# Loading w_mod by contraction rows in two parts, with zero products for the clock allowed from the first loads on, in a fused attention and MLP kernel

## The chip, the cores and the metric

The kernel runs on one core of one Trainium2 chip. The metric is the device time of one execution in microseconds. A second figure in this text is the **span**, from the first to the last instruction of the profile or of a timed run's record; the time is about 1.8 us longer than it (862.16 us against 860.4 in the profiled run of the kernel before). Every timed run, apart from the first six of the kernel before, also carries the mean clock that the throttle granted TensorE over the span.

## The reference, cut to what matters

One transformer block: x is 2048 rows by 640, 32 heads of 20, an MLP of 1536. What the change touches is the start, where six modulation vectors come from one product with w_mod (640 x 3840), and the first two of them scale and shift the normalised x ahead of the q/k/v projection.

```python
mod = (_silu(c) @ w_mod).reshape(c.shape[0], 6, 1, -1)
sa, ca, ga, sb, cb, gb = (mod[:, 0].copy(), mod[:, 1].copy(), ...)     # cut
h = _layernorm(x, axis=-1) * (1 + ca) + sa
x = x + ga * _A_ref(h, A_wqkv, A_wo)          # attention
h = _layernorm(x, axis=-1) * (1 + cb) + sb
x = x + gb * _B_ref(h, B_w1, B_b1, B_w2, B_b2)   # MLP
```

## The kernel before

The program does not write its instruction streams by hand. It lists operations with estimated durations, a list scheduler in the file gives each a time in a model of the chip, and the streams are emitted in the order of those times. Two consequences matter here. A number such as the byte count given to a load is only the scheduler's guess: the transfer itself does not depend on it, the order does. And where PE would idle in the model, the scheduler puts in zero products (name "fill") to keep TensorE's clock up.

The parts concerned, with cuts marked:

```python
OKT, RB = 3, 300000
# ... in the scheduler: when to put in a zero product
thin = 30.0 < bt < self.flast and not any(x.name == "fill" for x in avail["pe"]) and \
    sum(x[1] for x in fl if x[0] > bt - self.TICK + 0.3) < FLOOR
# ... the first loads (last argument: the scheduler's guess of bytes)
dma("sp", xb[0][:, 0:2, :], xsrc(0, 256), 560000)
dma("sp", xb[0][:, 2:4, :], xsrc(256, 256), 400000)
dma("sp", wm0[:, :, 0:D], wmod_v[:, :, 0:D], 1350000)
for a, b in ((D, WS), (WS, 2 * D)):
    dma("sp", wm0[:, :, a:b], wmod_v[:, :, a:b], 1280 * (b - a))
# ... 50 products of one column each, c after SiLU is s_col
for m in range(10):
    for kt in range(KD):
        mm((bb if m < WM else bb_)[:, m:m + 1], wm0[:, kt, m * 128:(m + 1) * 128], s_col[:, kt:kt + 1],
           kt == 0, kt == KD - 1, 0, 1, cyc=130, name="mod")
# ... their sums go to modc / modc2, with 1 added to the scale
# ... then transposes of the normalised x, evacuated with scale and shift; projections; scores; exponentials
# ... GpSimd clears the padded output weights, over the first x buffer once it has been normalised
pool(lambda e: e.memset(wo_pad[:, g, :], 0.0), [wo_pad[:, g, :]], [negh], dur=0.56, prio=7)
```

The softmax here doesn't subtract the row's maximum and nothing guards it: scores larger than these inputs give would overflow.

## Time and profile before

| | kernel before |
|---|---|
| time, median of 3 runs | 860.66 us (860.4 to 861.09) |
| span of the profiled run, mean clock | 860.4 us, 0.998 |
| ScalarE, PE, VectorE busy | 95%, 97%, 93% |
| first exponential | 20.69 us |

The prediction below shows the page, the chain and the clock. Here are the two timelines of the start. Columns: start in us, duration in us, engine, line, operation, output from input, shapes, count, and in brackets the idle time ahead with what ended it. PE, from the timeline of 7 to 24 us of the kernel before:

```profile
10.32 0.78 PE L753 MATMUL psum<-arena 128*128 128x1 bf16 x25 [1.04 <-DMA arena<-in_w_mod_dram]
11.72 0.53 PE L753 MATMUL psum<-arena 128*128 128x1 bf16 x15 [0.61 <-DMA arena<-in_w_mod_dram]
12.74 0.40 PE L753 MATMUL psum<-arena 128*128 128x1 bf16 x10 [0.42 <-DMA arena<-in_w_mod_dram]
13.01 0.89 PE L759 MATMUL psum<-arena 128*128 128x128 bf16 x13
```

The three groups of one-column products each wait for one part of w_mod; the transposes follow in the same queue. VectorE over the same stretch:

```profile
11.03 1.31 DVE L912 TENSOR_SCALAR arena<-arena 128x640 bf16<-128x640 bf16 x2 [1.99 <-POOL arena L908]
```

The last two x tiles are normalised by 12.34 us, so with the third part landing at 12.7 the two inputs of the transposes come at nearly the same time.

### The profile page before, as it was taken

Reading aid. Unit: us, or ns where it says so; the run is one execution under the profiler, and the core shown is the slowest. Engines: PE = TensorE matmul, PEld = TensorE weight load, DVE = VectorE, ACT = ScalarE, POOL = GpSimd, SP = SyncE. Lnnn points to the kernel's source line nnn. Section 1 sums busy time; section 2 is a strip of 40 time slices with the busy share of each in tenths; the row PEclk is TensorE's granted clock in tenths of the full one; section 3 lists DMA queues with packets and bytes.
Section 4 is the critical chain, followed back from the end, with each engine's and each line's share of the span. In section 5 each row is a group of like instructions: output and inputs, shape, how many; then the busy total and the mean of one; then the engine's idle time right before and its main releaser. Section 6 shows DMA issues by size and latency. Waiting matters only on the chain.

```text
span 860.4 us, 16684 instructions
## 1 busy us (share of the span) xinstructions
PE 836.7 (97%) x6710; PEld 296.0 (34%) x6768; DVE 797.5 (93%) x1601; ACT 821.5 (95%) x898; POOL 194.7 (23%) x460
## 2 busy tenths in 40 slices
PE   8999999999999999999999999999999999999998
PEld 3433333332332222333233333233333322333466
DVE  6958999999999999999999999999999999899862
ACT  2999999999999999999999999999999999999982
POOL 4500100027010000199300551000017400000110
PEclk9999999999999999999999999999999999999999
DMA  8600000011010000510000100100100000000000
GB/s 272 183 3 2 26 13 14 14 46 58 15 33 12 14 14 17 189 49 14 12 5 20 37 22 22 44 10 23 32 22 15 14 14 2 20 29 24 8 2 32
DMA packets 29320, 30.02 MB, mean 35 GB/s; under 512 B 10938, under 2 KB 23610, under 8 KB 29242
## 3 DMA queue, kind: packets, MB, share of 16 engines
q1 hardware_dynamic: 29242, 28.94, 10.6%
q8 instruction: 53, 0.87, 0.4%
q14 instruction: 25, 0.20, 0.1%
HBM read 25.94 MB, written 2.87 MB: 33 GB/s over the span
## 4 chain that ended last, share of the span: by engine, by line
PE 48%; ACT 37%; DVE 12%; DMA 1%; issue 1%; SPq 0%; ACTq 0%
ACT arena L1049 35%; PE psum L753 18%; PE psum L1032 18%; PE psum L1096 9%; DVE arena L1059 3%; DVE arena L1065 3%; PE psum L840 3%; DVE arena L1062 2%; ACT arena L1402 1%; DMA arena<-in_w_mod_dram 1%; PE psum L759 1%; DVE arena L900 1%; DVE arena L959 1%; DVE arena L977 1%; DVE arena L1395 0%
## 5 line engine op out<-in xcount | busy, mean ns | idle before, releaser
L1049 ACT ACTIVATE arena<-psum 128x1024 bf16<-128x1024 f32 x845 | 779.4, 1105 | 4.4 <-PE psum L1032 3.8
L1032 PE MATMUL psum<-arena 32*128 32x512 bf16 (+2 forms) x2304 | 367.6, 359 | 9.3 <-DVE arena L1065 2.7
L753 PE MATMUL psum<-arena 128*128 128x320 bf16 (+6 forms) x1708 | 328.3, 300 | 8.3 <-issue 3.9
L1059 DVE TENSOR_SCALAR arena<-psum 128x512 f16<-128x512 uint16 x356 | 236.2, 680 | 14.4 <-PE psum L1032 12.7
L1065 DVE SCALAR_TENSOR_TENSOR arena<-psum,arena 128x512 uint16<-128x512 f32 x356 | 237.6, 679 | 2.5
L1032 PEld LDWEIGHTS psum<-arena 32*128 32x128 bf16 x2304 | 98.7, 91 | 266.8 <-ACT arena L1049 188.0
L1096 PE MATMUL psum<-arena 128*32 128x512 bf16 (+5 forms) x2304 | 181.7, 362 | 1.2 <-DVE arena L1104 0.7
L753 PEld LDWEIGHTS psum<-arena 128*128 128x128 bf16 (+1 forms) x1766 | 126.9, 97 | 159.1 <-issue 105.1
L1144 POOL TENSOR_TENSOR arena<-arena 128x128 bf16<-128x128 bf16 x122 | 52.9, 463 | 484.0 <-DMA arena<-scr 484.0
L1062 DVE TENSOR_TENSOR arena<-arena 128x512 f16<-128x512 f16 x356 | 149.1, 437 | 1.5
L1096 PEld LDWEIGHTS psum<-arena 128*32 128x32 bf16 (+1 forms) x2304 | 44.3, 93 | 90.4 <-issue 78.7
L840 PE MATMUL psum<-arena 128*128 128x512 bf16 (+3 forms) x230 | 74.1, 394 | 0.0
L1313 POOL TENSOR_TENSOR arena<-arena 128x128 bf16<-128x128 bf16 x105 | 44.7, 459 | 38.3 <-DVE arena L1228 37.8
L1370 POOL TENSOR_TENSOR arena<-arena 128x128 bf16<-128x128 bf16 x120 | 50.7, 453 | 10.0 <-DVE arena L912 10.0
L900 DVE BATCH_NORM_STATS2 arena<-arena 128x6 f32<-128x320 bf16 x96 | 43.6, 479 | 1.1 <-DMA arena<-in_A_x_dram 0.6
L907 POOL TENSOR_SCALAR arena<-arena 128x1 f32<-128x1 f32 (+1 forms) x40 | 9.6, 241 | 106.8 <-DVE arena L902 106.6
L840 PEld LDWEIGHTS psum<-arena 128*128 128x128 bf16 x230 | 19.5, 100 | 35.7 <-issue 29.0
L1415 DVE TENSOR_TENSOR arena<-psum,arena 128x320 bf16<-128x320 f32 x32 | 15.5, 484 | 14.1 <-PE psum L753 14.0
L1395 DVE TENSOR_SCALAR arena<-psum,arena 128x512 bf16<-128x512 f32 (+1 forms) x39 | 28.1, 720 | 0.1
L959 DVE TENSOR_SCALAR arena<-psum,arena 128x512 bf16<-128x512 f32 x31 | 23.0, 742 | 4.7 <-PE psum L753 4.7
L912 DVE TENSOR_SCALAR arena<-arena 128x640 bf16<-128x640 bf16 x48 | 23.2, 497 | 3.0 <-POOL arena L908 3.0
L1104 DVE CAST arena<-psum 128x512 bf16<-128x512 f32 (+2 forms) x36 | 22.3, 621 | 3.3 <-PE psum L1096 3.3
(57 smaller groups left out, 215.0 us busy)
## 6 DMA issues: line engine op xcount, KB each, us to landing
arena<-scr SPq DMA_DIRECT2D x29, 256.0 KB
arena<-in_A_x_dram SPq DMA_DIRECT2D x6, 640.0 KB, 4.5
arena<-in_B_w_dram SPq DMA_DIRECT2D x2, 1920.0 KB
arena<-in_w_mod_dram SPq DMA_DIRECT2D x2, 1600.0 KB
out_dram<-arena SPq DMA_DIRECT2D x16, 160.0 KB, 1.8
arena<-in_A_wqkv_dram SPq DMA_DIRECT2D x3, 800.0 KB
arena<-in_A_x_dram SPq DMA_DIRECT2D x4, 320.0 KB
arena<-in_w_mod_dram SPq DMA_DIRECT2D x1, 800.0 KB
```

What stands on the lines that cost most here:

```text
L753: return P.op("pe", lambda e: e.matmul(outp, lhsT, rhs, start=start, stop=stop), R=[lhsT, rhs], W=[outp], dur=d, lat=d + 0.17, prio=prio, ...
L840: return lambda e: e.matmul(d_, zero, r_, start=new, stop=new, skip_group_check=True)
L900: dve(lambda e, hf=hf, xi=xi: e.bn_stats(s6[:, hf, :], xi), [xi], [s6[:, hf, :]], 320, prio=prio, dur=0.39)
L1032: r = e.matmul(o_, lh, rh, start=True, stop=True, tile_position=(32 * hl, 0))
L1049: return e.activation(ring3[:, s_[0]:s_[1] + 1:s_[1] - s_[0], :], src, ACTF.Exp, scale=ESC, bias=EBIAS)
L1059: d1 = P.op("dve", lambda e: e.tensor_scalar(vw_, m_, -65536.0 * QRHO, math.sqrt(QK2) / 65536.0, op0=ALU.add, op1=ALU.mult), dur=t_, lat=t ...
L1062: d2 = P.op("dve", lambda e: e.tensor_tensor(vw_, vw_, vw_, op=ALU.mult), dur=t2, lat=t2 + 0.095, prio=DP, name="d2", lock=True)
L1065: x.emit = lambda e: e.scalar_tensor_tensor(out=o_, in0=pb, scalar=QS0, in1=vw_, op0=ALU.add, op1=ALU.add)
L1096: r = e.matmul(o_, lh, rh, start=(kt == 0), stop=(kt == TT - 1), tile_position=(0, 32 * hl))
L1144: pool(lambda e, d1_=d1_, r1_=r1_: e.tensor_tensor(d1_, d1_, r1_, op=ALU.mult), [d1_], [d1_, r1_], dur=0.1 + 0.0021 * PSTEP, prio=3, name= ...
L1313: pool(lambda e, t_=t_, s_=s_, r_=r_: e.tensor_tensor(t_, s_, r_, op=ALU.mult), [t_], [s_, r_], dur=0.1 + 0.0021 * (b - a), prio=7)
L1370: pool(lambda e, op=op, t_=t_, r_=r_: e.tensor_tensor(t_, t_, r_, op=op), [t_], [t_, r_], dur=0.1 + 0.0021 * (b - a))
```

## The change

The intent: w_mod comes in two parts split by contraction rows, with 2560 contiguous bytes a row instead of 1280, 768 and 512; the partial sums of the first part wait in SBUF and VectorE adds those of the second; and zero products for the clock may stand anywhere from 4 us on, not from 30. The guess for the first q/k weights (RB) and the estimated length of a one-column product were changed too.

```diff
-WS = 1024
+E0, E1 = 1300000, 700000
-OKT, RB = 3, 300000
+OKT, RB = 3, 250000
+TH = 4.0
-                thin = 30.0 < bt < self.flast and ...
+                thin = TH < bt < self.flast and ...
-        dma("sp", wm0[:, :, 0:D], wmod_v[:, :, 0:D], 1350000)
-        for a, b in ((D, WS), (WS, 2 * D)):
-            dma("sp", wm0[:, :, a:b], wmod_v[:, :, a:b], 1280 * (b - a))
+        for a, b, eff in ((0, 3, E0), (3, KD, E1)):
+            dma("sp", wm0[:, a:b, :], wmod_v[:, a:b, 0:2 * D], eff)
...
+        for h, (a, b) in enumerate(((0, 3), (3, KD))):
+            bb = aux_bank()
+            for m in range(10):
+                for kt in range(a, b):
+                    mm(bb[:, m:m + 1], wm0[:, kt, m * 128:(m + 1) * 128], s_col[:, kt:kt + 1],
+                       kt == a, kt == b - 1, 0, 1, cyc=70, name="mod")
+            if h:
+                dve(lambda e, bb=bb: e.tensor_tensor(modc[:, 0:10], bb[:, 0:10], modc[:, 0:10], op=ALU.add), ...)
+            else:
+                ...   # copy columns 0 to 4, add 1 to columns 5 to 9
```

(modc2, which held the scales of the third part, is gone; the remaining lines of the diff follow from that.)

More of the change, by code (lines that the diff above doesn't have):

```diff
@@ L404, in schedule @@
                     fl.pop(0)
-                thin = 30.0 < bt < self.flast and not any(x.name == "fill" for x in avail["pe"]) and \
+                thin = TH < bt < self.flast and not any(x.name == "fill" for x in avail["pe"]) and \
                     sum(x[1] for x in fl if x[0] > bt - self.TICK + 0.3) < FLOOR
@@ L721, in bass_adaLN_cond__mha_block__mixer_channel_mlp__prompt_kernel @@
         modc = V(alloc(64), [16], F32)
-        modc2 = V(alloc(64), [16], F32)
         b1col = V(alloc(64), [KF], F32)
@@ L865, in bass_adaLN_cond__mha_block__mixer_channel_mlp__prompt_kernel @@
         dve(lambda e: e.tensor_copy(s_col, c_col), [c_col], [s_col], KD, prio=0)
-        bb, bb_ = aux_bank(), aux_bank()
-        WM = WS // 128
-        for m in range(10):
-            for kt in range(KD):
-                mm((bb if m < WM else bb_)[:, m:m + 1], wm0[:, kt, m * 128:(m + 1) * 128], s_col[:, kt:kt + 1],
-                   kt == 0, kt == KD - 1, 0, 1, cyc=130, name="mod")
-        dve(lambda e, bb=bb: e.tensor_copy(modc[:, 0:5], bb[:, 0:5]), [bb[:, 0:5]], [modc[:, 0:5]], 5, prio=0)
-        for b_, m0, m1 in ((bb, 5, WM), (bb_, WM, 10)):
-            dve(lambda e, b_=b_, m0=m0, m1=m1: e.tensor_scalar_add((modc if m0 == 5 else modc2)[:, m0:m1], b_[:, m0:m1], 1.0), [b_[:, m0:m1]],
-                [(modc if m0 == 5 else modc2)[:, m0:m1]], 5, prio=0)
+        for h, (a, b) in enumerate(((0, 3), (3, KD))):
[5 more added lines that the diff above has]
+            if h:
+                dve(lambda e, bb=bb: e.tensor_tensor(modc[:, 0:10], bb[:, 0:10], modc[:, 0:10], op=ALU.add),
+                    [bb[:, 0:10], modc[:, 0:10]], [modc[:, 0:10]], 10, prio=0)
+            else:
+                dve(lambda e, bb=bb: e.tensor_copy(modc[:, 0:5], bb[:, 0:5]), [bb[:, 0:5]], [modc[:, 0:5]], 5, prio=0)
+                dve(lambda e, bb=bb: e.tensor_scalar_add(modc[:, 5:10], bb[:, 5:10], 1.0), [bb[:, 5:10]],
+                    [modc[:, 5:10]], 5, prio=0)
         for w in (1, 0):
@@ L936, in tr_jobs @@
                     d = dst(kt, 1)
-                    s1, s2 = (modc if 5 + kt < WM else modc2)[:, 5 + kt:6 + kt], modc[:, kt:kt + 1]
+                    s1, s2 = modc[:, 5 + kt:6 + kt], modc[:, kt:kt + 1]
                     if engs[i] == "act":
```

## The prediction

> **What bounds the kernel now.** I read the page first, then the sums of twenty microseconds, then the first 40 us by single microseconds, by timeline and by chain.
>
> From the page of the kernel before, busy time and the chain that ended last:
>
> ```profile
> PE 836.7 (97%) x6710; PEld 296.0 (34%) x6768; DVE 797.5 (93%) x1601; ACT 821.5 (95%) x898; POOL 194.7 (23%) x460
> L1049 ACT ACTIVATE arena<-psum 128x1024 bf16<-128x1024 f32 x845 | 779.4, 1105 | 4.4 <-PE psum L1032 3.8
> ```
>
> ScalarE does 845 exponentials of 1024 columns, 779.4 us, and sat idle only 4.4 us in front of all of them. So from the first exponential on ScalarE is full (779.4/845 = 0.92 us each); PE and VectorE are nearly as full, but PE's share contains zero products. A change to the load of w_mod can only act before ScalarE fills up, or through a different order of instructions later. ScalarE's own timeline between 7 and 24 us (start, duration, what):
>
> ```profile
> 13.41 0.54 ACT L734 ACTIVATE arena<-arena 128x400 bf16<-128x400 bf16 x1 [10.38 <-DMA arena<-in_A_wqkv_dram]
> 13.86 2.10 ACT L734 ACTIVATE arena<-psum,arena 128x512 bf16<-128x512 bf16 x3
> 18.20 0.69 ACT L734 ACTIVATE arena<-psum,arena 128x512 bf16<-128x512 f32 x1 [2.25 <-PE psum L753]
> 20.69 1.02 ACT L1049 ACTIVATE arena<-psum 128x1024 bf16<-128x1024 f32 x1 [1.80 <-PE psum L1032]
> 22.39 1.94 ACT L1049 ACTIVATE arena<-psum 128x1024 bf16<-128x1024 f32 x2 [0.67 <-PE psum L1032]
> ```
>
> The first exponential starts at 20.69 us. What holds it is the chain of waits in the first 60 us:
>
> ```profile
> 3.20 9.49 DMA arena<-in_w_mod_dram
> 12.70 0.05 issue
> 12.74 0.40 PE psum L753 x10
> 13.14 0.75 PE psum L759 x13
> 13.89 1.53 PE psum L840 x4
> 15.42 0.22 issue
> 15.64 0.64 PE psum L753
> 16.28 0.43 PE psum L840
> 16.70 2.34 PE psum L753 x9
> ```
>
> The third part of w_mod lands at 12.7, ten products of one column follow, then 13 transposes of normalised x that stand behind them in PE's order, zero products (L840) while the transposes are evacuated, and the first projections. Those run slowly; the microsecond table (PE, PEld, DVE, ACT, POOL, then granted clock, DMA share, GB/s) says why:
>
> ```profile
> 11.00:12.00 1.00, 0.39 (x16) 0.30 (x13) 0.97 (x2) 0.00 (x0) 0.46 (x1) 1.00 0.67 171
> 12.00:13.00 1.00, 0.58 (x21) 0.44 (x19) 0.61 (x3) 0.00 (x0) 0.76 (x2) 1.00 0.79 168
> 14.00:15.00 1.00, 1.00 (x4) 0.39 (x3) 1.00 (x3) 1.00 (x2) 0.49 (x1) 0.50 1.02 371
> 15.00:16.00 1.00, 0.78 (x2) 0.30 (x2) 0.35 (x2) 0.95 (x2) 0.00 (x0) 0.50 1.06 369
> 16.00:17.00 1.00, 1.00 (x4) 0.38 (x3) 1.00 (x4) 0.00 (x0) 0.00 (x0) 0.50 1.04 371
> 34.00:35.00 1.00, 1.00 (x7) 0.31 (x5) 1.00 (x4) 1.00 (x2) 1.00 (x3) 1.00 1.03 412
> ```
>
> PE is mostly idle or on one-column products from 9 to 13 us; then the clock is halved for 14 to 17 us (with the edges 0.97 and 0.82 of the neighbouring rows, 3.4 us in all), exactly while the first projections are wanted.
>
> **What the Trainium skill says.** (1) "TensorE: Matmul & The Clock Gate", section "What's actually happening": half clock is the default and returns after an idle window of about 3.4 us; full clock comes after such a window of activity; a product of 512 columns goes at 426.7 ns cold and 215.7 ns warm. The trace agrees: weight loads of the zero products stand 0.43 us apart until 7.0 us, then six within 1.24 us, and the halved stretch is 3.4 us long. (2) "DMA: Bandwidth & Descriptors", section "Why small descriptors are slow (HBM only)": every packet has a fixed overhead. Here it agrees loosely: the w_mod parts of 384 and 256 columns (768 and 512 bytes a row) cross at 11 to 13 us, at 171 and 168 GB/s, while a later load of w_mod with 2560 bytes a row ran at 412 GB/s (34 to 35 us). But 1280-byte rows ran at 212 to 343 GB/s at 5 to 10 us and at some 365 at 18 to 24, so the early microseconds are slow for another reason as well. (3) "PSUM — Partial Sum Buffer", section "The four PSUM rules": a first product of a group clears the written marks of the whole bank. That is why the two halves cannot simply accumulate in one bank column by column, and are added on VectorE; no run here shows it yet. (4) "VectorE: DVE Perf Modes", section "The TRN2 errata", has a fixed cost per instruction: the trace's small VectorE operations take 0.16 to 0.17 us for 2 to 5 columns.
>
> **The change, part by part.**
>
> *The load.* Three column parts (rows of 1280, 768 and 512 bytes, 640 each, 1920 pieces in all) become two parts by contraction rows, 384 and 256 rows of 2560 bytes, 640 pieces for the same 1.64 MB. x (655 KB) goes ahead and is unchanged. If all of w_mod went at the 412 GB/s of the later load it would take 4.0 us and end near 6 + 4 = 10 us instead of 12.7. I do not believe all of it, because the early rate is low for 1280-byte rows too; the author's own guesses of effective bytes in the two versions (1350000 + 491520 + 327680 = 2.17 MB against 2.0 MB, at his 360 KB per us) differ by 0.47 us only. I take **1.1 us**, last landing at about 11.6. All later loads come about as much earlier: q/k weights (13.4), second x block (15.7).
>
> *The products.* 50 one-column products stay, at 0.78/25 = 0.031 us. After the last landing 20 are left instead of 10: 10 x 0.031 = **+0.3 us**, before the transposes.
>
> *VectorE.* Three small operations before (L872, L874 twice), three after: copy and add-one on the first half, now done before the last landing, and one addition of 10 columns after it, about 0.17 us against 0.16. **0.**
>
> *What then holds the transposes.* The normalisations of the last two x tiles end at 12.34 (11.03 + 1.31), behind GpSimd's power at 11.0. The transposes stood 13 deep behind the last mod products. With those done by 11.6 + 0.6 = 12.2, the transposes can end near 13.0 instead of 13.9: the load and the products together are worth 1.1 - 0.3 = **0.8 us**, and a still faster load hardly more.
>
> *The clock.* The scheduler's floor for zero products holds from 4 us on rather than 30. The gaps at 9.3 to 10.3, 11.1 to 11.7 and 12.3 to 12.7, and those among the mod products, get zero products, and the stretch of 3.4 us at half clock should go. Not all of its 1.7 us is on the path: until 15.96 (13.86 + 2.10) the projections wait for ScalarE's evacuations anyway. From 15.96 to 19.05 the path holds one zero product and nine projections, 3.1 us; ten at 0.216 would take 2.2 us, and if the products on the first four contraction tiles of q and k have gone before the last evacuation, five are left, 1.1 us. So 0.9 to 2.0, I take **1.4 us**. Against it: a zero product that PE has begun or that stands ahead in its order delays real work by 0.2 (warm) to 0.4 us (cold); I charge **0.2**.
>
> *Sum.* First exponential earlier by 0.8 + 1.4 - 0.2 = 2.0 us, near 18.7. The 0.67 us gap after it may shrink by some tenths, which I add as 0.3. From there ScalarE must stay full. It had 33 exponentials without a gap from 22.39 to 53.45 us, so there was supply, and the second x block comes earlier too. I let the whole 2.3 us through: 860.7 - 2.3 = **858.4 us**.
>
> **Rivals.** *A: the clock is kept but the path is ScalarE's and VectorE's.* The transposes' evacuations (0.70 us each, three in a row on ScalarE) and the normalisation on VectorE set the start. For it: 13.86 to 15.96 is unbroken ScalarE work, and the chain from 20 to 30 us is nearly all VectorE (statistics, normalisation). Then the gain is 0.8 to 1 us: 859.8. *B: the zero products get in the way.* They are put in by modelled times; where a load lands earlier than modelled, real work queues behind them, and at 20 to 30 us PE is already at 0.9 to 1.0 in the table. It would eat the gain: 860.5 to 862. *C: the reshuffle decides.* The order of all 16,684 instructions follows from the modelled start, so the share of exponentials on VectorE (356 half tiles) and the tail (20 us with ScalarE at 4.33 of 20) can move either way. One exponential pair moved to or from ScalarE is 0.92 us; I give this 2 us either way, on top of the rest. *D: the load gains the full 2.7 us and ScalarE starts near 17.5*: 857. Against it stand the normalisations, which end at 12.34 unless they too move.
>
> **Range and chances.** Centre 858.4; A and B together perhaps three in ten, D one in ten, C as a spread of about 2 us on everything: 855.2 to 861.0 should hold eight in ten. Two per cent is 17 us; the whole stretch before ScalarE fills is 22 us long, so neither side is in sight: faster 0.01, same 0.98, slower 0.01.
>
> **What would show it.** Right: granted clock 1.00 from 7 to 20 us; zero products between 9 and 13; last w_mod products starting between 11 and 12; first exponential at 18 to 19.3, with the exponentials' number and mean as before; every later stretch shifted by the same 2 us. Wrong in the load: last mod products at 12.5 or later. Wrong in the clock: 0.50 still in a row between 10 and 18, or clock 1.00 and the first exponential still after 20. Wrong in the carrying through: first exponential early, but idle time in front of L1049 grown well over 4.4 us, or the number of its instructions other than 845. The prediction as a whole is wrong if the end moves by more than the first exponential does.

## The result, and the profile after

| | before | after |
|---|---|---|
| median, 6 runs each | 860.79 us (859.11 to 861.47) | 859.9 us (859.19 to 861.97) |
| span and clock of the profiled run | 860.4 us, 0.998 | 860.1 us, 0.998 |
| first exponential in the profile | 20.69 us | 20.28 us |
| exponentials on ScalarE, idle ahead of them | 845, 4.4 us | 845, 4.6 us |

The ratio is 0.9995 with a 95% interval of 0.9981 to 1.0008. Ratios here are the mean time of one kernel's fast runs over that of the other's fast runs of the same rounds, so not quite the ratio of the medians quoted. Two later sets of the unaltered changed kernel gave 0.9988 (0.9973 to 1.0003) and 0.999 (0.9978 to 1.0003). Each of these intervals includes 1, so no set shows a gain by itself. Over all runs with a recorded span, taken together below, the two means differ by 0.8 us, give or take 0.5 by their spread, where 2.3 had been predicted.

PE in the profile of the changed kernel, from the timeline of 0 to 26 us:

```profile
10.22 0.90 PE L753 MATMUL psum<-arena 128*128 128x1 bf16 x30 [0.94 <-DMA arena<-in_w_mod_dram]
10.98 1.76 PE L839 MATMUL psum<-arena 128*128 128x512 bf16 x5
12.53 0.69 PE L753 MATMUL psum<-arena 128*128 128x1 bf16 x19
13.09 1.01 PE L839 MATMUL psum<-arena 128*128 128x512 bf16 x2
13.89 0.21 PE L753 MATMUL psum<-arena 128*128 128x1 bf16 x1
13.97 1.41 PE L759 MATMUL psum<-arena 128*128 128x128 bf16 x14
```

Five and two zero products (L839) stand among the modulation's products, and the transposes (L759) start at 13.97 us, later than the 13.01 of before. PE no longer stands idle for the second part of w_mod: it landed while the zero products ran, and the first weight load from it starts at 12.11. The table by microseconds of the same profile (PE, PEld, DVE, ACT, POOL, then clock, DMA share, GB/s) shows how they ran:

```profile
11.00:12.00 1.00, 1.00 (x9) 0.42 (x7) 0.81 (x4) 0.00 (x0) 0.07 (x2) 0.78 1.00 325
12.00:13.00 1.00, 1.00 (x18) 0.62 (x17) 0.74 (x1) 0.39 (x1) 0.99 (x2) 0.50 0.95 273
13.00:14.00 1.00, 1.00 (x13) 0.45 (x11) 0.00 (x0) 0.15 (x1) 1.00 (x3) 0.50 1.03 314
14.00:15.00 1.00, 1.00 (x13) 1.00 (x12) 0.36 (x2) 0.13 (x1) 0.14 (x1) 0.51 1.01 344
```

The half clock has not gone, it has moved: from 14 to 17 us to 11.6 to 15, where it stretches the zero products, the modulation and the transposes. Its length is the same as before: 0.22/0.5 + 1 + 1 + 0.49/0.5 = 3.42 us. ScalarE in the same profile:

```profile
14.87 2.12 ACT L734 ACTIVATE arena<-psum,arena 128x512 bf16<-128x512 bf16 x3 [1.72 <-PE psum L759]
20.28 1.02 ACT L1050 ACTIVATE arena<-psum 128x1024 bf16<-128x1024 f32 x1 [1.80 <-PE psum L1033]
```

The evacuations start one microsecond later than before (14.87 against 13.86), the projections then run at full clock and win it back, and 0.4 us are left. The end moved by 0.3 us. But of the six timed executions this profiled one is the only one with a mean clock of 0.998; the five others have 0.999 or 1.000 and spans of 857.4 to 858.7. That made the clock state the first thing to test.

### The profile page after: what moved, and what is told of

It is laid out like the page before. It is cut to its first block, busy times and chain, and to the rows that moved or that the text cites. A ratio compares the mean times of both kernels' runs of the same rounds, so it can differ in the third digit from the quotient of the medians.

```text
span 860.1 us, 16689 instructions
## 1 busy us (share of the span) xinstructions
PE 836.2 (97%) x6713; PEld 295.4 (34%) x6771; DVE 798.2 (93%) x1601; ACT 821.5 (96%) x898; POOL 194.8 (23%) x460
## 3 DMA queue, kind: packets, MB, share of 16 engines
q1 hardware_dynamic: 27946, 28.94, 10.6%
## 4 chain that ended last, share of the span: by engine, by line
ACT 41%; PE 39%; DVE 18%; DMA 1%; issue 1%; SPq 0%; ACTq 0%
ACT arena L1050 40%; PE psum L753 16%; PE psum L1033 14%; PE psum L1097 6%; DVE arena L1060 6%; DVE arena L1066 5%; DVE arena L1063 3%; PE psum L839 2%; DMA arena<-in_w_mod_dram 1%; DVE arena L960 1%; PE psum L759 1%; DVE arena L978 1%; DVE arena L1396 1%; DVE arena L1105 1%; ACT arena L1403 1%
## 5 line engine op out<-in xcount | busy, mean ns | idle before, releaser
L1033 PE MATMUL psum<-arena 32*128 32x512 bf16 (+2 forms) x2304 | 367.8, 359 | 9.6 <-DVE arena L1066 3.0
L1033 PEld LDWEIGHTS psum<-arena 32*128 32x128 bf16 x2304 | 98.2, 91 | 268.0 <-ACT arena L1050 188.9
L839 PE MATMUL psum<-arena 128*128 128x512 bf16 (+2 forms) x233 | 73.7, 388 | 0.0
L839 PEld LDWEIGHTS psum<-arena 128*128 128x128 bf16 x233 | 19.2, 98 | 34.6 <-issue 27.4
L1416 DVE TENSOR_TENSOR arena<-psum,arena 128x320 bf16<-128x320 f32 x32 | 15.5, 484 | 14.1 <-PE psum L753 13.9
L960 DVE TENSOR_SCALAR arena<-psum,arena 128x512 bf16<-128x512 f32 x31 | 23.0, 741 | 4.8 <-PE psum L753 4.8
```

The costliest lines, as they stand in the source:

```text
L839: return lambda e: e.matmul(d_, zero, r_, start=new, stop=new, skip_group_check=True)
L1033: r = e.matmul(o_, lh, rh, start=True, stop=True, tile_position=(32 * hl, 0))
```

## The experiments

Twelve experiments ran, each of four or five executions, in three batches with the kernel before beside each. In all of them, as above, 3.4 us at half clock show as a mean clock of 0.998 (3.42 x 0.5/860 = 0.002). The first 7 us do not show in this figure: the table reads clock 1.00 there, although the weight loads of the zero products stand 0.43 us apart until 7.0 us and closer afterwards. I call a run with 0.998 or less a half-clock run and one with 0.999 or more a full-clock run; both count as fast. (Two of the half-clock runs of before have 0.996, about twice as long a stretch; without them the mean of that kind is 859.51.) The experiments that take zero products out, add some or move a memset do so when the streams are emitted, after the schedule is made, so that the order of everything else stays as it was.

### again and again2: the changed kernel unaltered

Edit: none.

> The changed kernel once more, unaltered, for its spread and for a second profile. Theory 1 (zero products in the way): in the profile of the change seven zero products stand among the products of the modulation, at half clock, and the transposes start at 13.97 us instead of 13.01, so the earlier load is lost. [...]I expect mean clocks of 1.000 in most runs and 0.998 in a few, and 0.5 to 1.5 us between the two kinds. Theory 2 (rival: nothing changes at the start, the gain is lost later): the first exponential is 1 to 2 us early in the runs at full clock, but the end is not. Both expect 859.2 to 860.5 at full clock.

> The changed kernel unaltered, for the count of clock states and beside the other three of this batch. So far 9 of 11 executions kept the full clock (spans 857.4 to 858.7 us), the kernel before 5 of 18. Expected: 4 or 5 of 5 at 0.999 or more, mean span 858.0 to 858.6.

Measured: 859.8 and 859.97 us, medians of 5 runs each. Nine of these ten kept the full clock. With the first six that makes 14 of 16 for the changed kernel; of the kernel before, 27 executions with a recorded clock ran in the three batches, and 10 kept it. The spans, in us:

| | half clock | full clock | all |
|---|---|---|---|
| before | 859.65 (17 runs) | 858.12 (10) | 859.09 |
| changed | 859.85 (2) | 858.05 (14) | 858.27 |

In the same state no difference shows: 0.07 us at full clock, give or take 0.3, and 0.2 the other way at half, where the changed kernel has two runs only. What differs is how often the state comes. With the two means of the kernel before, going from 17 in 27 to 2 in 16 is worth (0.63 - 0.125) x 1.53 = 0.77 of the 0.82 us between the kernels.

The profile of again is of a full-clock run. PE, from the timeline of 7 to 24 us:

```profile
10.29 0.90 PE L753 MATMUL psum<-arena 128*128 128x1 bf16 x30 [0.67 <-DMA arena<-in_w_mod_dram]
11.05 1.24 PE L839 MATMUL psum<-arena 128*128 128x512 bf16 x5
13.06 0.94 PE L759 MATMUL psum<-arena 128*128 128x128 bf16 x14
```

and its first exponential:

```profile
18.91 1.02 ACT L1050 ACTIVATE arena<-psum 128x1024 bf16<-128x1024 f32 x1 [1.80 <-PE psum L1033]
```

Five zero products take 1.24 us here where they took 1.76; the transposes start at 13.06, still no earlier than the 13.01 of before. In again2, the same kernel and also at full clock, the first part of w_mod had landed at 9.66 us instead of 10.29, and PE, from its timeline of 7 to 24 us, starts them earlier behind the same zero products:

```profile
12.44 1.08 PE L759 MATMUL psum<-arena 128*128 128x128 bf16 x14
```

In the profile of again the first exponential is 1.78 us earlier than in the profile of before, and the end is 1.9 us earlier (858.5 against 860.4). So a gain near the predicted one exists between the profiles of again and before, but one of them is at half clock and the other is not. Theory 2 of the expectation, a gain lost later, falls: the end minus the first exponential is 839.7 in before, 839.8 in after, 839.6 in again and 839.7 in again2 (858.1 - 18.42).

### drop7: without the zero products among the modulation's products

```diff
 for o in self.streams.get(ename, []):
+    if o.name == "fill" and 9.0 < o.t0 < 11.9:
+        continue
     for d in waits[o.idx]:
```

> The changed kernel with the seven zero products among the modulation's products taken out at emission; the order of everything else is untouched. Theory 1 (zero products in the way): the last modulation products start when the second part has landed, about 11.5 us, the transposes when the last two tiles are normalised, about 12.8 instead of 13.97, and if the clock is full, the first exponential comes 0.8 to 1.2 us earlier than 20.28; the end moves by as much, to about 859. Theory 3 (the clock decides): without them the idle window returns, the half-clock stretch falls on the projections in all runs (mean clock 0.998), the first exponential is at 20.3 or later and the time 860.5 to 861, like the kernel before.

Measured: 860.41 us, five of five runs at half clock, mean span 858.54, ratio 0.9992 (0.998 to 1.0005). Both theories got a part. The half clock came back in every run, as theory 3 said; and still the first exponential came at 18.82 us, earlier even than the 19.1 to 19.5 that theory 1 had for full clock. PE from 7 to 24 us:

```profile
9.12 0.89 PE L757 MATMUL psum<-arena 128*128 128x1 bf16 x30
10.26 0.65 PE L757 MATMUL psum<-arena 128*128 128x1 bf16 x20 [0.25 <-DMA arena<-in_w_mod_dram]
11.54 0.23 PE L763 MATMUL psum<-arena 128*128 128x128 bf16 x1 [0.63 <-DVE arena L917]
12.41 1.57 PE L763 MATMUL psum<-arena 128*128 128x128 bf16 x13 [0.64 <-DVE arena L917]
```

In this run all of w_mod had landed by 10.26 us, and all transposes but one wait for the normalisation on VectorE (L917) to 12.41. Two things follow. First, this start is not all the work of the missing zero products: the first part of w_mod had landed by 9.12 us here and at 10.22 and 10.29 in after and again, and again2 started its transposes at 12.44 with the zero products in place. What they hold up is better read within one profile, from the end of the normalisation to the start of the transposes: 1.2 us in after, at half clock (12.75 to 13.97), 0.24 in again (12.82 to 13.06), nothing in again2. Second, behind them stands another bound at 12.4, so that the load's full gain of 2.4 us (12.7 to 10.3) could not have reached the transposes anyway. At half clock, the changed kernel without these zero products is 1.1 us better than the kernel before (858.54 against 859.65); with them its two half-clock runs are not better at all.

### before_warm and before_warm2: zero products alone, in the kernel before

```diff
     if o.name == "mod":
+        for _ in range({0: 4, 25: 2, 40: 1}.get(nmod, 0)):
+            self.filler(6, 512, False)(eng)
+        nmod += 1
```

> The kernel before, its order untouched, with seven more zero products where PE waits for the three parts of w_mod: four before the modulation's first product, two after the 25th, one after the 40th. Theory 4 (after the first batch: the change gains only by making the half-clock stretch rarer; at full clock both kernels span 858.2 and 858.0 us): mean clock 1.000 in all or nearly all runs, spans of 857.8 to 858.6 and a median of 859.7 to 860.3, so the zero products alone give the whole gain. If the earlier load gives a part: it stays at 860.3 or above, with full clock.

> The kernel before with seven more zero products at the waits for w_mod, once more, to lay it beside the changed kernel in the same rounds. If the clock is all that the change gives: same mean span as the changed kernel to 0.3 us. If the load in two parts gives something of its own: 0.4 us or more longer. The first time it had 858.6 against 858.0 of the changed kernel at full clock in another batch, so I lean to the second, with 0.3 to 0.6.

Measured: 860.34 and 860.52 us; ratios 0.9994 (0.9981 to 1.0007) and 0.9996 (0.9984 to 1.0009). All ten runs are at full clock, so seven zero products in the waits are enough to keep it. The mean span of the ten is 858.66. So zero products alone, with the old load, give about half of the gain: 0.43 us against all runs of the kernel before. But against those of its runs that kept the clock by chance they are 0.54 us worse. The second batch had the changed kernel beside it: 858.70 against 858.14 (5 runs each), so 0.6 us in favour of the rest of the change at equal clock, the upper end of what I had leant to.

Where that half microsecond lies can be looked up. From the timelines of 7 to 21 us of VectorE and PE of before_warm:

```profile
11.23 1.32 DVE L917 TENSOR_SCALAR arena<-arena 128x640 bf16<-128x640 bf16 x2 [1.99 <-POOL arena L913]
12.61 0.90 PE L764 MATMUL psum<-arena 128*128 128x128 bf16 x13
```

The transposes follow the end of the normalisation (12.55) at once, so the zero products do not hold them here. The first exponential is at 18.62 us in both profiles, between the 18.42 and 18.91 of the changed kernel, and the end follows it 839.9 and 840.2 us later, against 839.6 and 839.7. So these traces show neither a cost of the zero products nor a gain of the earlier load at the start. The difference comes later: the 33 exponentials from 20.3 us on take 31.07 and 30.86 us (31.06 in before), but 30.50 to 30.68 in after, again, again2, drop7, move7, clears_drop7 and clears_warm. That is 0.2 to 0.6 us in favour of the changed kernel whatever the clock at the start. Its cause is not shown; before_clears, with the old load, has 30.56 too.

One caution: the runs of before that keep the clock by chance may be those in which the loads came early and left a shorter gap. The timed runs have no trace, so this stays open, and with it how much of the 0.54 us is the zero products' own.

### load_only and floor_only: the halves of the change by their own switches

```diff
-TH = 4.0
+TH = 30.0        # load_only, in the changed kernel
```

```diff
-                thin = 30.0 < bt < self.flast and ...
+                thin = 4.0 < bt < self.flast and ...        # floor_only, in the kernel before
```

> The changed kernel with the floor for zero products back at 30 us: the load in two parts alone. The scheduler still puts five zero products between the two halves of the modulation, none after. If the load is what helps: transposes at 12.8 to 13.2, first exponential near 19.5, 859.5 us. If the clock is what helps: half clock during the projections as before, first exponential at 20.3 to 20.7 and 860.3 to 861.

> The kernel before with the floor for zero products from 4 us on, load in three parts. Twelve zero products then stand among the modulation's products. If zero products in the way cost and the clock gains: the transposes start near 14 us, later than 13.01, the clock is full from 14 on, first exponential near 20, 860 to 860.8. If only the clock counts: first exponential near 19 and 859.

Measured: load_only 870.99 us, ratio 1.0114 (1.0099 to 1.013), three of four runs fast with spans of 868.9 to 869.3 at full clock; the fourth, the profiled one, is slow (891.8 us, clock 0.969). floor_only 864.11 us, ratio 1.0035 (1.0023 to 1.0048), all at full clock. Neither expectation held: each half of the change alone is slower than the kernel before, by 10 and by 3 us, although in both the clock is full and the first exponential (18.43 and 20.14 us) is earlier than the 20.69 in the profile of before. The loss comes after the first exponential, where these switches change the order of instructions as well (floor_only even has 843 exponentials of 1024 columns instead of 845). So these two runs do not measure the halves. drop7 and before_warm, which keep the order, measure the zero products; no run measures the load in two parts alone in an unchanged order.

### after_rb: one of the scheduler's guesses put back

```diff
-OKT, RB = 3, 250000
+OKT, RB = 3, 300000
```

> The changed kernel with one number of the change undone: the scheduler's guess for the first q/k weights, 300000 again instead of 250000. It moves no transfer and adds no work; it only gives another order from about 15 us on. If the order of instructions after the start is settled by such guesses (as in the run with the load alone, which had the earliest first exponential, 18.43 us, and lost 10 us later): the first exponential stays within 0.5 us of 18.9 at full clock, but the end differs from the changed kernel by 2 us or more, likely later. If the order is harmless: 858 to 858.6.

Measured: 871.29 us, ratio 1.0121 (1.0105 to 1.0137); the four fast runs span 869.1 to 869.5 at full clock, a fifth was slow. The number changes no transfer and no work. The first exponential is at 18.89 us, the same as in again, and the end comes 10.6 us later. ScalarE, from the timeline of 18 to 880 us of after_rb:

```profile
35.97 1.94 ACT L1050 ACTIVATE arena<-psum 128x1024 bf16<-128x1024 f32 x2 [1.48 <-PE psum L1033]
41.76 10.19 ACT L1050 ACTIVATE arena<-psum 128x1024 bf16<-128x1024 f32 x11 [3.85 <-PE psum L1033]
```

and PE, from the timeline of 30 to 42 us:

```profile
35.54 0.39 PE L1033 MATMUL psum<-arena 32*128 32x512 bf16 x4 [0.15 <-DVE arena L960]
...
41.33 0.40 PE L1033 MATMUL psum<-arena 32*128 32x512 bf16 x4 [0.49 <-DVE arena L960]
```

Between 35.5 and 41.3 us PE has no scores (L1033) to give ScalarE: they wait for projections whose evacuation (L960) VectorE does late, at 39.4 and 40.4. Over the span ScalarE idles 12.4 us ahead of its exponentials instead of 4.6, which is 7.8 of the 10.6 us; another 1.7 are in the tail after its last exponential (869.1 - 834.9 against 858.5 - 825.95), and the rest was not traced. The slow profile of load_only has the same two gaps (1.86 us before 35.97 and 3.93 before 41.84), at full clock in that stretch. So the smaller RB belongs to the change: without it the other parts give an order that starves ScalarE.

### before_clears, clears_drop7, clears_warm: the normalisation out of the way

```diff
 def emit(self):
     ops = self.ops
+    st = self.streams["pool"]
+    early = [o for o in st if o.name == "clear" and o.t0 < 13.0]
+    for i, o in enumerate(early):
+        o.t0, o.t1 = 13.5 + 0.65 * i, 13.5 + 0.65 * (i + 1)
+    st.sort(key=lambda o: o.t0)
+    ...                                      # renumbered
```

(The memsets are given the name "clear" for this.) before_clears is the kernel before with this, clears_drop7 is drop7 with it, and clears_warm has zero products put back besides: three before the first and two before the 31st modulation product, three after the transposes.

> The kernel before with four GpSimd memsets of the padded output weights moved from 8.6 to 13 us behind the last work that the first 512 rows need from GpSimd, order otherwise untouched. They delay the power for x tiles 3 and 4 by 0.9 us[...]. Expected: the normalisation of the last two tiles ends near 11 us instead of 12.34, and nothing else moves, because the third part of w_mod lands at 12.7 here: the first exponential and the time stay within 0.4 us of the kernel before in the same clock state. If it gains over 1 us, the load was not what held the transposes.

> The changed kernel without the seven zero products among the modulation's products and with the four memsets moved. In the run without the seven, both parts had landed by 9.1 and 10.3 us and the transposes waited for the normalisation until 12.4. Expected if that was the bound: normalisation ends at 11 to 11.5, transposes at 11 to 12, first exponential 0.8 to 1.2 us earlier than 18.82, so near 17.8; the clock may be half at 11 to 15 and then take back up to 0.7. Span 857.0 to 858.0, time 859.0 to 859.8.

> As the run before, with zero products put back where PE waits: three before the first and two before the 31st product of the modulation, three more after the transposes. Expected: mean clock 1.000 in all runs, transposes near 11.5, first exponential 17.2 to 17.8, span 856.8 to 857.4, time 858.6 to 859.2. If the clock stays half or the first exponential is later than 18.5, the zero products again stand in the way.

Measured: 861.19, 860.14 and 859.93 us; ratios 1.0007 (0.9993 to 1.002), 0.9991 (0.9978 to 1.0003) and 0.9989 (0.9977 to 1.0002). In before_clears the normalisation ends at 11.20 instead of 12.34, its two tiles taking 0.80 us instead of 1.31, and PE still waits for the third part of w_mod, to 12.07 in this profile: here the load holds the transposes. The median does not move, as expected, but not every part of the expectation held. The first exponential came 0.6 us earlier (20.09), as much as the third part landed earlier, and the two full-clock runs span 859.1 and 859.4, about 1.1 us more than those of the kernel before. So an unmoved time may be a gain and a loss that cancel. The memsets did harm in their new place, from the timelines of VectorE and GpSimd of before_clears:

```profile
13.69 2.56 DVE L895 COPY arena<-arena 128x400 bf16<-128x400 bf16 x1
13.77 2.34 POOL L1307 MEMSET arena<- 128x640 bf16 x4
```

A copy of 0.27 us took 2.56, as long as all four memsets. "SBUF — State Buffer" in the Trainium skill, section "SBUF: two separate sides", says that the port pair shared by VectorE and GpSimd is locked for a whole instruction. The trace agrees as far as it shows a copy as long as the memsets beside it; if the lock is the cause, VectorE waited for four in a row.

With the earlier load the move does reach the transposes. From the timeline of 7 to 21 us of PE in the profile of clears_drop7, a full-clock run:

```profile
11.22 0.65 PE L764 MATMUL psum<-arena 128*128 128x1 bf16 x20 [0.82 <-DMA arena<-in_w_mod_dram]
11.74 0.94 PE L770 MATMUL psum<-arena 128*128 128x128 bf16 x14
```

The first exponential is at 17.84 us and the span 857.3, the shortest seen. But the other four of its five runs are at half clock, with 858.2 to 859.2. With zero products put back (clears_warm) five of five keep the clock, and the mean span is 858.18, no better than the changed kernel at full clock: the second part of w_mod landed at 12.03 us in that profile, after 10.26 in drop7 and 11.22 in clears_drop7. Expected were 856.8 to 857.4; this missed. The first exponential (18.55) lay just past the 18.5 that was to mean zero products in the way, but ahead of the last modulation products PE stood idle for w_mod, behind no zero product.

### move7: the same number of zero products, elsewhere

```diff
+    if o.name == "fill" and 9.0 < o.t0 < 11.9:
+        continue
+    # and 4 before the first, 1 before the 31st, 2 after the last modulation product
```

> The changed kernel with its seven zero products moved: four before the modulation's first product, one before the 31st, two after the last one, where PE waits for w_mod or for the normalisation; the order otherwise untouched. Theory 1 (they stood in the way): full clock in all runs, transposes at 12.4 to 12.7 instead of 13.06, first exponential at 18.2 to 18.6 instead of 18.91, mean span 857.5 to 857.9. Rival (the landing of the loads and the normalisation hold the transposes, and the zero products stand beside that): no change to the changed kernel at full clock, 858.0.

Measured: 859.92 us, ratio 0.9989 (0.9977 to 1.0002), five of five at full clock, mean span 858.08. The rival holds in the time: 858.08 against 858.05 of the changed kernel at full clock. The profile by itself would have fitted theory 1 (transposes at 12.68, first exponential at 18.53), but again2 reached 12.44 and 18.42 with the zero products where they were. PE from 8 to 21 us:

```profile
11.74 0.65 PE L765 MATMUL psum<-arena 128*128 128x1 bf16 x20 [0.56 <-DMA arena<-in_w_mod_dram]
12.68 0.94 PE L771 MATMUL psum<-arena 128*128 128x128 bf16 x14
```

At full clock the zero products are not what is left: the landing (11.74 here) and the normalisation (which ended at 12.56) put the transposes near 12.5 in any case. In all, move7 and clears_warm kept the clock in ten runs of ten, the changed kernel in 14 of 16. They beat the kernel before in the mean by 0.9 to 1.0 us and the changed kernel by 0.1 to 0.2, which is within what these rounds can tell.

## Why the prediction was right or wrong

The time lay in the range (859.9 in 855.2 to 861.0), and "within 2%" was right, which at 17 us either way was hardly in doubt. The size of the gain was not: 2.3 us predicted, about 0.8 measured. By the prediction's own signs the profile of the change read "wrong in the load" (19 of the last modulation products start at 12.53) and "wrong in the clock" (0.50 in the rows from 12 to 14); the profile of again, at full clock, read right in the clock, with a first exponential at 18.91, in the 18 to 19.3 expected.

**Where ScalarE fills up, and carrying through: right.** In all profiles with the order of before or after, the end follows the first exponential at 839.5 to 840.2 us (before_clears alone, with its stalled copy, at 838.8), the number of exponentials stayed 845 and the idle time ahead of them 4.1 to 4.7.

**The clock: the mechanism and the size were right, its certainty failed.** I took 1.4 us as a sum to be gained. The states of before are 1.53 us apart, and from ScalarE's first evacuation of a transpose to the first exponential it is 6.83 us in the profile of before against 5.26 and 5.25 in again and again2. But "the stretch of 3.4 us at half clock should go" treats one profile as the kernel. Before has that stretch in 17 runs of 27, the changed kernel in 2 of 16 (one of them its profile), so the term is worth 0.77 on average. The profile of before was also a late one of its kind: 860.4 where its half-clock runs average 859.65.

**The load: mis-sized, and the step after it failed.** I expected the last landing at 11.6 instead of 12.7. But 12.7 was a late draw. With three parts the first weight load from the last of them starts at 12.74 in the profile of before, and at 12.06, 12.11 and 12.07 in before_warm, before_warm2 and before_clears. With two parts it starts at 12.11, 12.03, 11.39, 10.26, 11.22, 11.73 and 12.03 (after, again, again2, drop7, clears_drop7, move7, clears_warm). That is 12.2 against 11.5 on average, 0.7 us where I took 1.1, with a spread of 0.7 us within the first kind and of 1.9 within the second.

What failed is "the transposes can end near 13.0 instead of 13.9", the 0.8 us of the part on what then holds the transposes. In the three profiles of the changed kernel they started at 13.97, 13.06 and 12.44 and ended at 15.38, 14.00 and 13.52; with the old load at full clock (before_warm) they ended at 13.51. Both rivals have a part in this. Rival A named the normalisation as the next bound: it ended at 12.35 to 12.82 in the unaltered and drop7 profiles. I had not seen that the copies of the first half would now stand ahead of it in VectorE's order (11.16 and 11.36 us in the profile after, normalisation from 11.44 instead of 11.03). Rival B named the zero products: at half clock they held the transposes 1.2 us beyond the normalisation (after), and the spans differ by 1.3 us (859.85, two runs, against 858.54 of drop7), where I had charged 0.2. At full clock the 0.2 was enough: 0.24 us in again, nothing in again2, and moving them changed no time (move7).

**The gap after the first exponential: wrong.** I added 0.3 us for it; it stayed 0.67. What became shorter is the stretch behind it, the 33 exponentials named under before_warm, by 0.2 to 0.6 us, for a reason that is not shown.

**The reshuffle: mis-sized by far.** I gave rival C 2 us either way. One guess of the scheduler alone moves the end by 10.6 us at an unchanged start, and each half of the change by its own switch costs 3 and 10. That the whole change shows none of this is because the guess was set with it.

**The skill's pages.** The window of about 3.4 us in "TensorE: Matmul & The Clock Gate", section "What's actually happening", fits the half-clock stretches that I measured (3.42 us). The same section says that the window runs freely, which may be why the state varies from run to run; no run here shows it, and landings that vary by over a microsecond would do the same. The rule of "PSUM — Partial Sum Buffer", section "The four PSUM rules", that a first product clears the marks of the whole bank, was not tested: no run accumulates both halves in one bank. My reading of the slow 11 to 13 us was too narrow: the q/k weights, with rows of 320 bytes, are queued right behind w_mod, and in again, with w_mod in rows of 2560 bytes, the rate also fell to 214 GB/s at 12 to 13 us.

**What stays open.** Whether the lucky full-clock runs of before had earlier loads; why before_warm ends about half a microsecond later than other full-clock runs, and why the 33 exponentials are shorter in the changed kernel; why the landing of the same two loads varies by 1.8 us between runs; how much activity in a window is enough to keep the clock; and what the changed estimate for a one-column product does to the order by itself, which no run tried.

## What to carry to other kernels

Before counting a clock stretch in a profile as time to be won, look at the mean clock of all timed runs: the profile shows one draw, and a change may only alter the odds. A landing time in one profile is a draw as well. Zero products in a queue that is emitted in order can stand in front of the very data that a faster load delivers: here by 1.2 us in a half-clock profile, by 0.24 or nothing at full clock, where moving them into the waits gained no time. And where a scheduler makes the order, test a part of a change with the order held fixed, because switching the part off by its constant measures the new order instead (here 10 us against an effect under one).

## What the Trainium skill lacked or had wrong

- "TensorE: Matmul & The Clock Gate" says that an idle window throttles, not how much work counts as idle. In the profile after, PE was marked busy for 0.44, 0.28 and 0.78 of the microseconds from 8 to 11, with 30 products of one column among them, and half clock still began at 11.6; seven products of 512 columns spread over the waits kept the full clock in ten runs of ten.
- The same page tells of the run-to-run spread in warming up, not of the way back: the unaltered kernel before, with PE mostly idle or on one-column products from 9 to 13 us, fell to half clock in 17 runs of 27, worth 1.53 us each.
- "DMA: Bandwidth & Descriptors" gives rates and fixed costs, no spread for the first loads of a program: the same second part of w_mod, fifth in the queue, landed at 10.26 to 12.03 us in the four profiles where PE stood waiting for it (drop7, clears_drop7, move7, clears_warm).
- "SBUF — State Buffer" describes the lock between VectorE and GpSimd for one instruction. In before_clears a copy that took 0.27 us in before lasted 2.56, through four memsets in a row; no page says that the waiting engine may lose again at each next instruction.
